# RWKV-6 attention and a GELU MLP: the last tile's first product by seven half products, and a new order at the start

## The chip, the cores and the metric

The kernel runs on one core of one Trainium2 chip. A core has a matrix engine (TensorE, PE in the profile, with its weight loads shown apart as PEld), a vector engine (VectorE, DVE), a scalar engine (ScalarE, ACT), GpSimd (POOL) and a queue engine that issues DMAs (SyncE, SP). Each engine works through its own queue in order, and waits for the others by semaphores. Matmuls write only to PSUM, an on-chip buffer of eight banks of 512 fp32 columns; VectorE and ScalarE read the results from there. The metric is the device time of one execution in microseconds (us); less is better. 13 runs of the kernel before gave a median of 614.05 us (610.53 to 616.07).

## The reference

Two stages: a linear attention with a decaying state per head (RWKV-6), and an MLP with the exact GELU on its output.

```python
for t in range(S):                                   # per batch and head
    cur = np.einsum('bhd,bhe->bhde', u[None] * kt, vt)
    y[:, :, t] = np.einsum('bhd,bhde->bhe', rt, state + cur)
    state = wt[:, :, :, None] * state + np.einsum('bhd,bhe->bhde', kt, vt)
...
h = x @ w_in                                         # x: y as (3072, 384)
g = 0.5 * h * (1.0 + erf(h * inv_sqrt2))
return (g @ w_out).astype(np.float32)
```

Sizes: batch 4, 8 heads, 768 steps, head size 48, so x is 3072 x 384; w_in is 384 x 2048, w_out 2048 x 384. The weights come as float64 and are turned into fp32 on the chip; everything is computed in fp32.

## The kernel before

The 3072 rows are cut into eight tiles x = 0 to 7 of T = 384 steps. For each tile `attention(x, unit)` makes x transposed (`xT`, three chunks of 128 of the 384 inputs by 384 rows), and `mlp(x)` multiplies it by w_in (h, line 723), applies GELU (line 726) into `g`, and multiplies by w_out. Both are Python generators: each `yield` ends a piece of work, and the loop at line 902 pulls the pieces of `mlp(x - 1)` one by one (a "step") and puts pieces of the next tile's attention between them, at the steps that the lists `place` and `place_next` name. The order in which the code runs is the order in every engine's queue; semaphores are placed by the framework from the tiles that an instruction reads and writes.

**h of a tile** (lines 718 to 739): sixteen groups f of 128 of the 2048 columns; each takes three fp32 matmuls of 128 x 128 by 384 columns, over the three chunks, into a PSUM tile `h_ps` of one bank (two such buffers, tag "mm"), and one GELU.

**The product with w_out** for tiles from 1 on (lines 768 to 810): two of the three blocks of 128 rows are multiplied by seven products of halves in place of eight (Strassen's way in Winograd's form), with sums of g in `s1`, `s2`, `s3` (lines 730 to 738) and sums of w_out made once (`w_sums`). Each product is eight matmuls of 192 columns. The third block of an odd tile waits and is paired with that of the even tile after it; that of the last tile is alone and is multiplied plainly at the very end (lines 849 to 865: 16 matmuls of 384 columns, a copy on VectorE, a store of 192 KB).

**Tile 0's attention** runs in two units of two head pairs each, before any MLP work; `units.reverse()` at line 885 puts unit 1 (pairs 2 and 3) first for the last pieces. Those are: the state chain on VectorE (lines 602 to 618), the first half of y with a small "fence" copy on VectorE (lines 630 to 634), and the second half of y (line 648), whose results are copied to xT: unit 0 by lines 653 to 657, unit 1's pair 3 through `ysb` and six DMAs (lines 671 to 676), and its pair 2 by two VectorE copies (line 669). Then the conversion of weights (`convert`, 16 pieces, VectorE lines 303 to 310, ScalarE lines 291 and 292) is mixed with the steps of `mlp(0)` and with tile 1's attention. In that attention `halves` makes six levels; at each, matmuls (line 402) go to a tile `d`, VectorE scales r (line 437) and writes to a_sb under a mask (line 447); the diagonal is one more set of products (lines 409 and 413).

**From tile 2 on** the attention uses `quarters`: ScalarE and VectorE lay out r in kx (lines 488, 493, 494), then come small matmuls (508, 515) at step 8 and step 13, VectorE scales and masked copies (522 to 553), the state chain at step 18 and the two halves of y at steps 20 and 21. PSUM tiles of the attention have two banks each, tag "d", three buffers: together with the two of tag "mm" they fill the eight banks.

Of the kernel before, what the change touches and what calls it, by code (L numbers as in the profile page):

```python
# [10 lines left out]
F32 = mybir.dt.float32  # L11
# [5 lines left out]
AF = mybir.ActivationFunctionType  # L17
# [6 lines left out]
T = 384  # L24
# [7 lines left out]
BANK = 512  # L32
# [12 lines left out]
def kernel(  # L45
# [25 lines left out]
    nc = tc.nc  # L71
    NX = rkw.shape[0]
    NP = u.shape[1]
    NPART = NP // Q
    N_TOK, DM = out.shape
    HALVES = 2
    NJ = DM // 128
    DF = w_in.shape[1]
    NF = DF // 128
# [4 lines left out]
    io = ctx.enter_context(tc.tile_pool(name="io", bufs=2))  # L84
    wk = ctx.enter_context(tc.tile_pool(name="wk", bufs=2))
# [15 lines left out]
    ALL = NP * T  # L101
# [85 lines left out]
    def keep_warm(n):  # L187
        t = ps.tile([128, BANK], F32, name="warm", tag="mm", bufs=2) if n else None
        for _ in range(n):
            nc.tensor.matmul(t, lhsT=zeros[:, 0:128], rhs=zeros, start=True, stop=True)  # L190
# [121 lines left out]
    xT_of = {}  # L312

    def attention(x, unit):
# [346 lines left out]
        for b in reversed(range(np_)):  # L661
            for q in reversed(range(Q)):
                pair = parts[b] * Q + q
                y = ys[b][:, :, q * N3 * C:(q + 1) * N3 * C].rearrange("p c (i t) -> p c i t", t=C)
                if pair < NJ:
                    for z in range(2):
                        s = slice(z * G, z * G + D)
                        copy = nc.vector.tensor_copy if x == 0 else nc.scalar.copy
                        copy(out=xT[s, pair, :].rearrange("p (i c t) -> p c i t", c=2, t=C), in_=y[s])
                    continue  # L670
                ysb = wk.tile([128, T], F32, name="ysb", bufs=1)
                nc.scalar.copy(out=ysb.rearrange("p (i c t) -> p c i t", c=2, t=C), in_=y)
                for z in range(2):
                    for j in range(NJ):
                        e = z * G + j * (G - D)
                        (nc.scalar if z * NJ + j > (2 if x == 0 else 3) else nc.sync).dma_start(out=xT[z * G + D:(z + 1) * G, j, :], in_=ysb[e:e + G - D, :])
# [12 lines left out]
    def w_sums():  # L689
# [3 lines left out]
        for i, (x, y) in enumerate((((0, 1), (0, 0)), ((1, 1), 0), ((1, 1), (0, 1)), ((1, 0), 1))):  # L693
            for k in range(2):
                ks = slice(k * FG, (k + 1) * FG)
                nc.vector.tensor_sub(sums[i][:, ks], w_quarter(*x, k), sums[y][:, ks] if isinstance(y, int) else w_quarter(*y, k))
                yield

    def mlp(x):


# [12 lines left out]
        def new_sums(tag):  # L714
            return cv.tile([128, FG, 128], F32, name="s", tag=tag)

        s1, s2, s3 = [], [], []
        for n, group in enumerate((0, 2, 1, 3) if halves else range(4)):
            gs[group] = gp.tile([128, FG, T], F32, name="g")
            for f in range(group * FG, (group + 1) * FG):  # L720
                h_ps = ps.tile([128, BANK], F32, name="h_ps", tag="mm", bufs=2)[:, 0:T]
                for j in range(NJ):
                    nc.tensor.matmul(h_ps, lhsT=w_in_sb[:, f // FI, j, f % FI * 128:(f % FI + 1) * 128], rhs=xT[:, j, :],  # L723
                                     start=(j == 0), stop=(j == NJ - 1))
                t = T - 128 if waits else T
                nc.scalar.activation(out=gs[group][:, f % FG, 0:t], in_=h_ps[:, 0:t], func=AF.Gelu)  # L726
                if waits:
                    nc.scalar.activation(out=alone[:, f], in_=h_ps[:, t:], func=AF.Gelu)

                if halves and n == 3 and f % FG >= FG - 2:  # L730
                    k = f % FG - FG + 2
                    for s, tag in ((s1, "f"), (s2, "e")):
                        s.append(new_sums(tag))
                    s3.append(s3_sb[0][:, k * FG:(k + 1) * FG])
                    a00, a10, a11 = (gs[g][:, :, a:a + 128] for g, a in ((k, 0), (k, 128), (k + 2, 128)))
                    nc.vector.tensor_add(s1[k], a10, a11)  # L736
                    nc.vector.tensor_sub(s2[k], s1[k], a00)
                    nc.vector.tensor_sub(s3[k], a00, a10)
                yield

        def product(o, lhs, rhs, start=False):
# [19 lines left out]
        def psum():  # L761
            return ps.tile([128, BANK], F32, name="o_ps", tag="mm", bufs=2)[:, 0:HM]

        def two_rows():
            return [wk.tile([128, DM], F32, name="o_sb", bufs=2) for _ in range(2)]


        if halves:
# [44 lines left out]
        if waits:  # L813
            _, o2, o1 = psum(), psum(), psum()
            o_sb = wk.tile([128, DM], F32, name="o_sb", bufs=2)
            product(o2, of_alone(0), of_w(0, 0), True)
            nc.scalar.copy(out=p1_alone, in_=o2)
            yield
            product(o1, of_alone(1), of_w(1, 0), True)
            nc.vector.tensor_add(o_sb[:, 0:HM], o1, p1_alone)  # L820
            store(row0 + 256, o_sb[:, 0:HM])
            yield
        elif ends:
            o_sb = two_rows()
            p1, u2, u3 = p1_alone, *(wk.tile([128, HM], F32, name=name, bufs=1) for name in ("u2", "u3"))
            o2, o1 = psum(), psum()
            product(o1, of_blocks(2, 1), of_t(3), True)
            nc.scalar.copy(out=o_sb[1][:, 0:HM], in_=o1)
            yield
            product(o2, of_sums(s2), of_t(1), True)  # L830
            nc.vector.tensor_add(u2, o2, p1)
            yield
            product(o1, of_sums(s1), of_t(0), True)
            nc.scalar.copy(out=o_sb[1][:, HM:], in_=o1)
            for k in range(2):
                nc.vector.tensor_sub(s2[k], alone[:, HF + k * FG:HF + (k + 1) * FG], s2[k])
            yield
            product(o2, of_sums(s3), of_t(2))
            nc.vector.tensor_add(u3, o2, p1)
            for c in range(2):  # L840
                z = o_sb[1][:, c * HM:(c + 1) * HM]
                nc.vector.tensor_add(z, z, u3)
            store(row0 + 256, o_sb[1])
            yield
            product(o1, of_sums(s2), of_w(1, 1))
            nc.vector.tensor_add(o_sb[0][:, 0:HM], o1, u2)
            store(row0 - T + 256, o_sb[0][:, 0:HM], HM)
            yield
        else:

            if halves:
                psum()
            for blocks in ((2,),) if halves else ((0, 1), (2,)):
                o_ps = [ps.tile([128, BANK], F32, name="o_ps", tag="mm", bufs=2)[:, 0:DM] for _ in blocks]
                for f in range(NF):
                    for i, o in zip(blocks, o_ps):
                        nc.tensor.matmul(o, lhsT=block(i, f // HF, f % HF), rhs=w_out_sb[:, f, :],  # L857
                                         start=(f == 0), stop=(f == NF - 1))
                    if (not halves or f % 4 == 3) and f < NF - 1:
                        yield  # L860
                for i, o in zip(blocks, o_ps):
                    o_sb = wk.tile([128, DM], F32, name="o_sb", bufs=2)
                    nc.vector.tensor_copy(out=o_sb, in_=o)
                    store(x * T + i * 128, o_sb)
                yield
# [23 lines left out]
    for _ in shares:  # L889
        pass  # L890
    convert()
    for unit, warm in zip(units, ((1, 2, 1), (0, 0, 5))):
        for n in warm:
            next(unit)
            keep_warm(n)
    convert()
    slots = attention(1, 0)
    next(slots)
# [2 lines left out]

    for x in range(1, NX):

        place = [1, 2, 4, 7, 9, 11, 13, 15, 18, 20, 26, 32] if x == 1 else [1, 6, 8, 13, 15, 16, 18, 18, 20, 21]
        place_next = [38, 47] if x == 1 else [21, 24] if x % 2 == 0 else [25, 27]
        loads = load(x + 1, nc.scalar if x > 1 else nc.sync)

        times = range(20, 30) if x == 1 else (2, 3, 4, 5, 16, 17, 18, 19, 20, 21)
        following = attention(x + 1, 0) if x + 1 < NX else iter(())
        more = iter(())  # L910
        for step, _ in enumerate(mlp(x - 1)):
            if x == 1 and step == 2 * NF - 2:

                make_quarter_masks()
                more = w_sums()
            next(more, None)
            if x == 1 and step in (0, 2, 4, 6, 8, 10, 12, 14, 15, 17, 18, 20, 22, 24):
                convert()
            if step in times:
                next(loads, None)  # L920
            while place and place[0] <= step:
                place.pop(0)
                next(slots, None)
            while place_next and place_next[0] <= step:
                place_next.pop(0)
                next(following, None)
        for _ in slots:
            pass
        slots = following
# [62 lines left out]
```

## Time and profile before

| | us |
|---|---|
| median of 13 runs | 614.05 |
| the profiled execution | 614.72 |
| its span, first to last instruction | 612.9 |
| TensorE busy | 592.9 |
| VectorE busy | 448.3 |
| ScalarE busy | 173.5 |
| start to the first h matmul | 50.05 |
| first h matmul of the last tile | 549.65 |
| its h, in the chain that ended last | 30.96 |
| its seven products | 18.20 |
| its third block | 10.33 |

The page gives for each engine its busy time, and then the chain of work that ended last, followed back from the last instruction. The timeline lists instructions in order of time, merged where they are alike; in brackets is the idle time of the engine before them and what ended it. The granted TensorE clock was 0.999 of full speed over the run.

### The profile page before, as it was taken

What the parts mean: (1) busy time and instruction counts of PE and PEld (TensorE: products, weight loads), DVE (VectorE), ACT (ScalarE), POOL (GpSimd) and SP (SyncE); (2) the same over time, 40 slices, a digit from 0 to 9 for tenths busy, and PEclk for the clock granted to TensorE, in tenths of its full rate; (3) what the DMA queues carried; (4) which work ended last, traced back from release to release, by engine and by line L of the source; (5) the groups of instructions that cost most, each with busy time, mean ns of one, the idle gap of its engine ahead of it and who ended that gap; (6) DMA issues with size and microseconds to landing.
All of it is one profiled execution on the core that took longest, in us unless ns stands there. A gap on an engine that the chain in (4) does not pass through costs nothing.

```text
span 612.9 us, 15812 instructions
## 1 busy us (share of the span) xinstructions
PE 592.9 (97%) x6917; PEld 446.5 (73%) x6935; DVE 448.3 (73%) x801; ACT 173.5 (28%) x389; POOL 8.4 (1%) x24
## 2 busy tenths in 40 slices
PE   8768899999999999999999999999999999999997
PEld 4455566566699568996689668995789668995694
DVE  7868999999885988679776888569786888520120
ACT  2236367123322232113222232023322132022200
POOL 3100000000000000000000000000000000000000
PEclk9999999999999999999999999999999999999999
DMA  5756358203042303213052203213052002010001
GB/s 195 212 202 206 109 158 290 76 30 91 2 110 72 97 1 77 89 35 90 2 109 72 75 24 74 88 39 91 3 107 73 8 2 40 18 40 0 1 1 40
DMA packets 50565, 46.71 MB, mean 76 GB/s; under 512 B 31680, under 2 KB 35904, under 8 KB 50496
## 3 DMA queue, kind: packets, MB, share of 16 engines
q1 hardware_dynamic: 33152, 29.31, 15.8%
q10 hardware_dynamic: 17344, 16.39, 9.9%
q8 instruction: 55, 0.90, 0.6%
q14 instruction: 14, 0.11, 0.1%
HBM read 36.24 MB, written 4.72 MB: 67 GB/s over the span
## 4 chain that ended last, share of the span: by engine, by line
PE 81%; DVE 13%; issue 3%; DMA 2%; ACT 1%; SPq 0%; DVEq 0%
PE h_ps L723 35%; PE o_ps L743 29%; PE d L515 4%; PE o_ps L857 4%; DVE e L306 2%; DVE rkw L437 2%; PE y_ps L648 2%; PE kv_ps L592 2%; PE y_ps L630 2%; DVE a_sb L447 1%; DVE w_out_sb L310 1%; DMA rkw<-kx 1%; DMA rkw<-in_rkw_dram 1%; PE d L508 1%; PE d L402 1%
## 5 line engine op out<-in xcount | busy, mean ns | idle before, releaser
L723 PE MATMUL h_ps<-xT,w_in_sb 128*128 128x384 f32 x768 | 254.2, 489 | 1.2 <-ACT f L291 1.2
L723 PEld LDWEIGHTS h_ps<-xT,w_in_sb 128*128 128x128 f32 x768 | 144.1, 190 | 98.3 <-ACT f L291 1.7
L726 ACT ACTIVATE g<-h_ps 128x384 f32<-128x384 f32 (+1 forms) x128 | 57.3, 450 | 198.8 <-PE h_ps L723 198.8
L743 PE MATMUL o_ps<-t,s 128*128 128x192 f32 x480 | 81.9, 329 | 0.0
L743 PEld LDWEIGHTS o_ps<-t,s 128*128 128x128 f32 x480 | 77.8, 190 | 0.7
L546 DVE COPY_PREDICATED a_sb<-quarter,d 128x384 f32<-128x384 uint8 (+2 forms) x108 | 45.0, 438 | 2.5
L857 PE MATMUL o_ps<-w_out_sb,g 128*128 128x384 f32 x128 | 43.0, 490 | 0.1
L743 PE MATMUL o_ps<-w_out_sb,g 128*128 128x192 f32 x224 | 38.7, 326 | 0.0
L743 PEld LDWEIGHTS o_ps<-w_out_sb,g 128*128 128x128 f32 x224 | 37.0, 190 | 1.9
L857 PEld LDWEIGHTS o_ps<-w_out_sb,g 128*128 128x128 f32 x128 | 23.7, 190 | 16.7 <-DVE w_out_sb L310 1.0
L736 DVE TENSOR_TENSOR s<-g 128x512 f32<-128x512 f32 x14 | 9.4, 670 | 29.1 <-ACT g L726 29.1
L402 PEld LDWEIGHTS d<-rkw 64*64 64x64 f32 x1152 | 19.0, 136 | 13.9 <-issue 7.0
L743 PE MATMUL o_ps<-w_out_sb,s 128*128 128x192 f32 x160 | 28.3, 330 | 0.0
L743 PE MATMUL o_ps<-t,g 128*128 128x192 f32 x160 | 27.6, 326 | 0.0
L402 PE MATMUL d<-rkw 64*64 64x64 f32 (+1 forms) x1152 | 21.5, 223 | 6.2 <-DVE a_sb L447 2.5
L339 DVE TRANSPOSE_TENSOR_REDUCE rkw<-kx 128x48 f32<-128x1536 f32 (+3 forms) x24 | 26.8, 1155 | 0.2
L515 PEld LDWEIGHTS d<-kx,rkw 64*64 64x64 f32 x1152 | 24.3, 133 | 3.4 <-DVE a_sb L553 1.6
L515 PE MATMUL d<-kx,rkw 64*64 64x96 f32 x1152 | 26.5, 245 | 0.0
L743 PEld LDWEIGHTS o_ps<-t,g 128*128 128x128 f32 x160 | 26.3, 190 | 0.0
L743 PEld LDWEIGHTS o_ps<-w_out_sb,s 128*128 128x128 f32 x160 | 25.9, 190 | 0.4
L528 DVE TENSOR_TENSOR rkw<-rkw,tot_sb 128x768 f32<-128x768 f32 x12 | 11.5, 958 | 17.4 <-PE d L515 17.4
L375 DVE TENSOR_TENSOR rkw<-rkw 128x384 f32<-128x384 f32 (+2 forms) x24 | 23.6, 1008 | 0.4
(117 smaller groups left out, 642.4 us busy)
## 6 DMA issues: line engine op xcount, KB each, us to landing
rkw<-in_rkw_dram ACTq DMA_DIRECT2D x45, 256.0 KB, 2.8
raw<-in_w_out_dram SPq DMA_DIRECT2D x8, 768.0 KB, 4.5
out_dram<-o_sb SPq DMA_DIRECT2D x21, 192.0 KB, 1.9
raw<-in_w_in_dram SPq DMA_DIRECT2D x5, 768.0 KB, 5.4
v_in<-in_v_dram ACTq DMA_DIRECT2D x5, 584.0 KB, 3.7
raw<-in_w_in_dram SPq DMA_DIRECT2D x9, 256.0 KB, 4.1
rkw<-in_rkw_dram SPq DMA_DIRECT2D x8, 288.0 KB, 3.6
rkw<-in_rkw_dram SPq DMA_DIRECT2D x9, 256.0 KB, 7.4
```

The lines of the kernel that those rows point to most:

```text
L306: nc.vector.scalar_tensor_tensor(out=e, in0=hi, scalar=0x80000000, in1=e, op0=ALU.bitwise_and, op1=ALU.bitwise_or)
L339: nc.vector.tensor_reduce(out=fine_sb[:, e, 0:n].rearrange("p a n -> p (a n)"), in_=kx[:, o:o + n * n_m].rearrange("p (m j) -> p m j", j=3 ...
L375: nc.vector.tensor_mul(z, z, by)
L402: nc.tensor.matmul(d[half[p], g, n * width:(n + 1) * width], lhsT=kc[half[g], b, i, p], rhs=right(half[g], b, i, p), start=True, stop=True)
L437: nc.vector.tensor_mul(rk, rk, tt)
L515: nc.tensor.matmul(d[half[p], g, i * 3 * C // 2:(i + 1) * 3 * C // 2], lhsT=kc[half[g], (n + i) // NI, (n + i) % NI, p], rhs=rx[half[g], 2 ...
L546: nc.vector.copy_predicated(out=an[:, :, :, :, (a + 1) * h:], mask=mask.to_broadcast(data.shape), data=data)
L592: nc.tensor.matmul(kv_ps[half[g], p, i * D:(i + 1) * D], lhsT=k_t(b, i, p, g), rhs=vs(b, i, g)[half[p], 0:D], start=True, stop=True)
L723: nc.tensor.matmul(h_ps, lhsT=w_in_sb[:, f // FI, j, f % FI * 128:(f % FI + 1) * 128], rhs=xT[:, j, :], start=(j == 0), stop=(j == NJ - 1))
L726: nc.scalar.activation(out=gs[group][:, f % FG, 0:t], in_=h_ps[:, 0:t], func=AF.Gelu)
L743: nc.tensor.matmul(o, lhsT=lhs(j), rhs=rhs(j), start=start and j == 0, stop=(j == HF - 1), skip_group_check=True)
L857: nc.tensor.matmul(o, lhsT=block(i, f // HF, f % HF), rhs=w_out_sb[:, f, :], start=(f == 0), stop=(f == NF - 1))
```

## The change

At the start, unit 1 of tile 0 yields once more, between the copies of pair 3 and of pair 2, and the last pieces of the two units are pulled in another order: unit 0's state chain comes before the copies of unit 1's pair 2. In the list `place` for tile 1 the steps 2 and 4 become 3 and 5.

For the last tile, h is computed for its 384 rows in two halves of 192 columns: over the first two of the three chunks of inputs, pairs of groups (f and f + 8) take seven products of halves in place of eight, and the third chunk is added plainly, four matmuls, in the same accumulations. That is eleven matmuls of 192 columns for a pair, where there were six of 384. `h_sums` makes the sums of w_in (eight VectorE operations of 128 x 512) and of x (four of 128 x 192) during the steps of the tile before; `h_halves` issues the matmuls and the additions into six PSUM banks, taken as three tiles of two banks. `of_g` holds the sums of g that stood inline. The third block's product is moved ahead of the seven products, with its last two f at its end.

The diff, without blank lines and the parts that only re-indent:

```diff
@@ attention
         for b in reversed(range(np_)):
             for q in reversed(range(Q)):
                 pair = parts[b] * Q + q
+                if x == 0 and pair == NP - 2:
+                    yield
@@ after w_sums
+    HT = T // 2
+    in_s, in_t = [], []
+    def h_sums():
+        n = DF // 2
+        rest = io.tile([128, v.shape[2]], F32, name="v_in")
+        for z in (bufs[0][:, 0:n], rest[:, 0:n], kx[:, 0:n], bufs[1][:, ALL:ALL + n]):
+            in_s.append(z.rearrange("p (i c) -> p i c", c=WI))
+        hi = DF // WI // 2
+        def w(a, c, k):
+            return w_in_sb[:, a * hi + k * hi // 2:a * hi + (k + 1) * hi // 2, c, :]
+        def s(i, k):
+            return in_s[i - 1][:, k * hi // 2:(k + 1) * hi // 2]
+        for i in range(4):
+            for k in range(2):
+                if i == 0:
+                    nc.vector.tensor_add(s(1, k), w(1, 0, k), w(1, 1, k))
+                elif i == 1:
+                    nc.vector.tensor_sub(s(2, k), s(1, k), w(0, 0, k))
+                elif i == 2:
+                    nc.vector.tensor_sub(s(3, k), w(0, 0, k), w(1, 0, k))
+                else:
+                    nc.vector.tensor_sub(s(4, k), w(0, 1, k), s(2, k))
+                yield
+        in_t.extend(tot_sb[:, i * HT:(i + 1) * HT] for i in range(4))
+        xT = xT_of[NX - 1]
+        x00, x01, x10, x11 = (xT[:, c, b * HT:(b + 1) * HT] for c in range(2) for b in range(2))
+        nc.vector.tensor_sub(in_t[0], x01, x00)
+        nc.vector.tensor_sub(in_t[1], x11, in_t[0])
+        yield
+        nc.vector.tensor_sub(in_t[2], x11, x01)
+        nc.vector.tensor_sub(in_t[3], x10, in_t[1])
+        yield
@@ mlp
+        def of_g(k):
+            for s, tag in ((s1, "f"), (s2, "e")):
+                s.append(new_sums(tag))
+            s3.append(s3_sb[0][:, k * FG:(k + 1) * FG])
+            a00, a10, a11 = (gs[g][:, :, a:a + 128] for g, a in ((k, 0), (k, 128), (k + 2, 128)))
+            nc.vector.tensor_add(s1[k], a10, a11)
+            yield
+            nc.vector.tensor_sub(s2[k], s1[k], a00)
+            yield
+            nc.vector.tensor_sub(s3[k], a00, a10)
+            yield
+        def h_halves():
+            banks = [ps.tile([128, 2, BANK], F32, name="d", tag="d", bufs=3) for _ in range(3)]
+            b_1, b_6, b_7, b_5, b_4, b_0 = (z[:, i, 0:HT] for z in banks for i in range(2))
+            temps = [bufs[1][:, 2 * ALL + i * HT:2 * ALL + (i + 1) * HT] for i in range(8)]
+            x00, x01, x10, x11 = (xT[:, c, b * HT:(b + 1) * HT] for c in range(2) for b in range(2))
+            more = iter(())
+            for f in range(HF):
+                k = f // FG
+                if f % FG == 0:
+                    for group in (k, k + 2):
+                        gs[group] = gp.tile([128, FG, T], F32, name="g")
+                p1, u2, u3 = (wk.tile([128, HT], F32, name=name, bufs=1) for name in ("p1", "u2", "u3"))
+                u5, c12, c21, c22 = temps[f % 2::2]
...
+                last = [xT[:, 2, b * HT:(b + 1) * HT] for b in range(2)]
+                multiply(b_1, (w(0, 0), x00))
+                nc.scalar.copy(out=p1, in_=b_1)
+                multiply(b_6, (s(2), in_t[1]))
+                nc.vector.tensor_add(u2, b_6, p1)
+                multiply(b_7, (s(3), in_t[2]))
+                nc.vector.tensor_add(u3, b_7, u2)
+                multiply(b_5, (s(1), in_t[0]))
+                nc.vector.tensor_add(u5, b_5, u3)
+                multiply(b_1, (w(0, 1), x10), (w(0, 2), last[0]), start=False)
+                gelu(0, 0, b_1)
+                multiply(b_4, (w(1, 1), in_t[3]), (w(1, 2), last[0]))
+                nc.vector.tensor_add(c21, b_4, u3)
+                gelu(1, 0, c21)
+                multiply(b_0, (w(1, 2), last[1]))
+                nc.vector.tensor_add(c22, b_0, u5)
+                gelu(1, 1, c22)
+                multiply(b_5, (s(4), x11), (w(0, 2), last[1]), start=False)
+                nc.vector.tensor_add(c12, b_5, u2)
+                gelu(0, 1, c12)
+                next(more, None)
+                if f % FG == FG - 1:
+                    more = of_g(k)
+            for _ in more:
+                pass
...
+        final = x == NX - 1
+        if final:
+            h_halves()
-        for n, group in enumerate((0, 2, 1, 3) if halves else range(4)):
+        for n, group in enumerate(() if final else (0, 2, 1, 3) if halves else range(4)):
...
+        if final:
+            o_ps = ps.tile([128, BANK], F32, name="o_ps", tag="mm", bufs=2)[:, 0:DM]
+            order = [f for f in range(NF) if f % HF < HF - 1] + [HF - 1, NF - 1]
+            for n, f in enumerate(order):
+                nc.tensor.matmul(o_ps, lhsT=block(2, f // HF, f % HF), rhs=w_out_sb[:, f, :], start=(n == 0), stop=(n == NF - 1))
+            o_sb = wk.tile([128, DM], F32, name="o_sb", bufs=2)
+            nc.scalar.copy(out=o_sb, in_=o_ps)
+            store(x * T + 256, o_sb)
+            yield
...
-        else:
-            if halves:
-                psum()
-            for blocks in ((2,),) if halves else ((0, 1), (2,)):
+        elif not final:
+            for blocks in (0, 1), (2,):
@@ the order at the start
-    for unit, warm in zip(units, ((1, 2, 1), (0, 0, 5))):
-        for n in warm:
-            next(unit)
-            keep_warm(n)
+    for unit, n in ((0, 1), (0, 2), (0, 1), (1, 0), (0, 0), (1, 0), (1, 4)):
+        next(units[unit])
+        keep_warm(n)
@@ the loop over tiles
-        place = [1, 2, 4, 7, 9, 11, 13, 15, 18, 20, 26, 32] if x == 1 else [1, 6, 8, 13, 15, 16, 18, 18, 20, 21]
+        place = [1, 3, 5, 7, 9, 11, 13, 15, 18, 20, 26, 32] if x == 1 else [1, 6, 8, 13, 15, 16, 18, 18, 20, 21]
...
-            next(more, None)
+            if x == NX - 1 and step == 2:
+                more = h_sums()
+            if x < NX - 1 or step in (2, 3, 4, 5, 17, 19, 22, 23, 24, 26):
+                next(more, None)
```

More of the change, by code (lines that the diff above doesn't have):

```diff
@@ new lines, in h_halves, with w, s, multiply @@
+        def h_halves():
[11 more added lines that the diff above has]
+                u5, c12, c21, c22 = temps[f % 2::2]
+                def w(a, j):
+                    g = a * HF + f
+                    return w_in_sb[:, g // FI, j, g % FI * 128:(g % FI + 1) * 128]
+                def s(i):
+                    return in_s[i - 1][:, f // FI, f % FI * 128:(f % FI + 1) * 128]
+                def multiply(o, *factors, start=True):
+                    for i, (lhsT, rhs) in enumerate(factors):
+                        nc.tensor.matmul(o, lhsT=lhsT, rhs=rhs, start=start and i == 0, stop=(i == len(factors) - 1),
+                                         skip_group_check=True)
+                def gelu(a, b, z):
+                    nc.scalar.activation(out=gs[2 * a + k][:, f % FG, b * HT:(b + 1) * HT], in_=z, func=AF.Gelu)
+                last = [xT[:, 2, b * HT:(b + 1) * HT] for b in range(2)]
[23 more added lines that the diff above has]
+                pass
@@ L730, in mlp @@
                 if halves and n == 3 and f % FG >= FG - 2:
[L731 to L738, printed above, removed]
+                    for _ in of_g(f % FG - FG + 2):
+                        pass
                 yield
@@ L858, in mlp @@
                                          start=(f == 0), stop=(f == NF - 1))
-                    if (not halves or f % 4 == 3) and f < NF - 1:
+                    if f < NF - 1:
                         yield
```

## The prediction

> **What bounds the kernel now.** I read the page first (busy shares, then the chain that ended last), then the timeline of the last tile, of the tile before it and of the start, where the change works.
>
> ```profile
> PE 592.9 (97%) x6917; PEld 446.5 (73%) x6935; DVE 448.3 (73%) x801; ACT 173.5 (28%) x389; POOL 8.4 (1%) x24
> PE 81%; DVE 13%; issue 3%; DMA 2%; ACT 1%; SPq 0%; DVEq 0%
> ```
>
> TensorE is 81% of the chain; VectorE's 13% is nearly all in the first 118 us, where it converts weights. So a stall of TensorE after 118 us is paid in full, and before that VectorE's chain is what counts. The timeline of the last tile (start, length, engine, line; in brackets the idle time before and its releaser):
>
> ```profile
> 549.65 31.12 PE L723 MATMUL h_ps<-xT,w_in_sb 128*128 128x384 f32 x96
> 555.66 0.49 ACT L726 ACTIVATE g<-h_ps 128x384 f32<-128x384 f32 x1 [1.44 <-PE h_ps L723]
> ...
> 583.41 0.32 ACT L774 COPY p<-o_ps 128x192 f32<-128x192 f32 x1 [2.11 <-PE o_ps L743]
> ...
> 588.41 7.96 PE L743 MATMUL o_ps<-t,s 128*128 128x192 f32 x48
> ...
> 596.41 0.36 DVE L792 TENSOR_TENSOR u<-o_ps,p 128x192 f32<-128x192 f32 x1 [3.57 <-PE o_ps L743]
> ...
> 598.81 10.48 PE L857 MATMUL o_ps<-w_out_sb,g 128*128 128x384 f32 x32
> ...
> 609.34 0.56 DVE L863 COPY o_sb<-o_ps 128x384 f32<-128x384 f32 x1 [9.96 <-PE o_ps L857]
> ```
>
> There are two hardware instructions to one fp32 matmul of the code (96 for 16 x 3). The chain has L723 at 30.96 us for 96, so 0.3225 us each, and L743 at 18.20 for 112, so 0.1625 each: a matmul of 192 columns costs 0.325 us, half of one of 384. A reader of PSUM starts 0.20 us after the slot of the last matmul ends (596.21 to 596.41); a copy of 192 columns takes 0.32 on ScalarE, an add 0.36 on VectorE. TensorE idles nowhere in this stage.
>
> The start, where VectorE has the lead:
>
> ```profile
> 42.38 0.48 ACT L672 COPY ysb<-y_ps 128x384 f32<-128x384 f32 x1 [3.16 <-PE y_ps L648]
> ...
> 42.89 1.12 DVE L669 COPY xT<-y_ps 48x384 f32<-48x384 f32 x2 [2.21 <-ACT ysb L672]
> 44.03 0.26 DVE L617 COPY st<-kv_ps 128x96 f32<-128x96 f32 x1
> 44.32 1.84 DVE L606 SCALAR_TENSOR_TENSOR st<-st,tot_sb,kv_ps 128x48 f32<-128x48 f32 x10
> ...
> 46.08 0.15 DVE L634 COPY fence<-y_ps 128x2 f32<-128x2 f32 x1
> ...
> 46.29 1.38 PE L648 MATMUL y_ps<-rkw,st 64*64 64x64 f32 x40 [2.78 <-DVE fence L634]
> ...
> 47.72 0.96 ACT L656 COPY xT<-y_ps 48x384 f32<-48x384 f32 x2 [4.86 <-PE y_ps L648]
> ...
> 48.71 1.12 DVE L656 COPY xT<-y_ps 48x384 f32<-48x384 f32 x2 [2.48 <-ACT xT L656]
> ```
>
> Two things: VectorE idles 2.21 us before L669 although the state chain (L617, L606) behind it had its inputs at 37.5 (the kv matmuls of 36.61 had ended). And the second L656 waits for the first, although ScalarE reads the first bank of that y_ps and VectorE the second. The writes aren't the reason: they interleave without overlap in xT, and the next view shows such writes running at once. So **the program's waits hold a PSUM tile of two banks as one thing**: an access to one bank waits for another engine's access to the other.
>
> The tile before the last (kx is written there by L488 and L493, interleaved, and both start at 492.54):
>
> ```profile
> 492.54 1.34 ACT L488 COPY kx<-rkw 128x384 f32<-128x384 f32 x3 [1.74 <-DVE rkw L375]
> 492.54 0.56 DVE L493 TENSOR_TENSOR kx<-rkw,tot_sb 128x384 f32<-128x384 f32 x1
> 493.50 0.96 DVE L494 TENSOR_TENSOR kx<-kx,tot_sb 128x768 f32<-128x768 f32 x1 [0.40 <-ACT kx L488]
> ...
> 494.08 1.06 PE L508 MATMUL d<-rkw 64*128 64x48 f32 x16
> ...
> 495.07 2.21 PE L515 MATMUL d<-kx,rkw 64*64 64x96 f32 x96
> ```
>
> VectorE works from 476.83 to 494.46 without a gap but that of 0.40, and L515 needs L494: only 0.6 us of slack there.
>
> **What the Trainium skill says.** "Perfetto Trace Analysis", Matmuls: independent matmul groups should rotate through PSUM banks, so that the evacuation of one overlaps the next. L723 does so (two tiles of one bank), and shows no idle TensorE. "PSUM — Partial Sum Buffer", Terms: two engines on one bank at once is an error, reads included. That explains L669 behind L672 (same banks), not the two L656, which sit in different banks; there the trace decides.
>
> **The change, part by part.**
>
> *Start.* The chain of the second unit moves ahead of L669: it runs from 40.70 (after the first unit's fence, 40.52+0.16) to 42.83, inside the old gap; L669 still starts at 42.89 and ends at 44.01; the fence comes at 44.03, not 46.08, and L648 at 44.25, not 46.29 (its other input, L630, is done by 43.5). Both L656 and the conversion behind them follow: 2.04 us earlier. ScalarE's xT DMAs are issued by 45.03, before its L656 at 45.68; the last lands about 2.2 later, 47.2, before h starts at 48.0. One warm-up matmul fewer lies in idle time. From there to 118 VectorE is the chain and keeps its order, since steps 3 and 5 fall between the same conversions (even steps) as 2 and 4. TensorE gets one h group ahead of each moved slot, which removes its 1.59 us wait at 65.03, but it then waits for the next L437 instead: nothing more. **-2.04.**
>
> *Tile before the last.* h_sums puts four VectorE operations of 128x512 at steps 2 to 5, behind L375 and ahead of L493. L736 to L738 have this form: 0.61 us from one to the next. 4 x 0.61 = 2.44, so L493 starts at 495.0, L494 at 495.54 and ends at 496.50 (the gap of 0.40 is swallowed). L515 starts at 496.56, not 495.07. **+1.49**, all of it TensorE, and all behind it shifts together. Bounds: 0 if these operations found a gap, 2.4 if the gap of 0.40 stays. The later ones lie in idle time: s3 ahead of L610 (520.93 to 521.54, and L615 waits for kv until 522.08), then behind L783, with 1.16 idle before the fence; s4 and in_t between 538 and 549, in gaps of 3.64, 3.64 and 1.53.
>
> *h of the last tile.* Per pair of f: 11 matmuls of 192 for 12, 3.575 us; eight make 28.60 against 30.96, 2.36 less, if nothing waits. But banks are paired b_1+b_6, b_7+b_5, b_4+b_0, each a tile "d" of the kind seen in L656. In program order TensorE then waits three times per f (0.05 us from release to restart, as from ScalarE's 2.24 to the first warm-up at 2.29):
> - b_6 after the copy of b_1. That copy stands on ScalarE behind the gelu of c12 of the f before: last b_5 slot ends at 0; +0.20+0.36 (c12) +0.03+0.33 (gelu; 0.27 for 128 columns, 0.38 for 256) +0.32 (copy) +0.05 = 1.29, where b_6 was due at 0.325: **0.96** (in the first f, with ScalarE free, 0.20+0.32+0.05 = 0.57).
> - second b_5 product after u3 (reads b_7). b_6 ends at 1.615, +0.20+0.36 (u2), +0.03+0.36 (u3), +0.05 = 2.615; due at 1.94: **0.67**.
> - b_0 after c21 (reads b_4): 0.20+0.36+0.05 = **0.61**.
>
> Sum 2.24 per f. Restart: L723's first twelve after a pause take 4.11 where 11 x 0.3225+0.489 = 4.04, so 0.07 each; bounds 0 and 0.19 (a whole weight load, PEld's mean). Period 3.575+2.24+0.21 = 6.03; first 5.64; total 5.64+7 x 6.03 = 47.9. Against 30.96: **+16.9** (15.2 to 19.8). The sums of of_g (0.65 each) fall behind c12, while VectorE waits for b_6. VectorE's six adds and ScalarE's five operations, 2.2 and 1.6 us per f, are no bound by themselves.
>
> *Rest.* The third block's product (10.33) moves ahead of the seven (18.20): same work; its 14 first matmuls (9 us) cover the last gelus. The end is an add of 0.36 in place of the copy of 0.56, with a store of the same size: **-0.2**.
>
> Sum: -2.04+1.49+16.9-0.2 = +16.2 on the profiled execution's 614.72 us (span 612.9). The median of the runs shown is 614.05, so **630.2 us**.
>
> **Rivals.**
> 1. *Banks are held apart* (faster): the wait of the second L656 comes from xT after all. Then no wait in h binds: the copy of b_1 ends at 1.24, before the accumulation at 1.30. -2.04+1.49-2.36-0.2 = -3.1: 611.0. For it: the copies do write one xT. Against: L488 and L493. It decides as soon as b_6 need not wait for the copy of b_1; even 0.4 us per f would eat it.
> 2. *Each restart costs a full weight load*: 24 x 0.12 = +2.9: 633.1. For it: no view shows 128x128 weights loaded ahead over a wait.
> 3. *The start gives nothing*: another input of h is late (its idle of 1.20 there is put down to ScalarE's L291, which is none of its inputs), or weights' DMAs hold the earlier conversions: 632.2.
> 4. *The pairing holds only in part*, so that one of the three waits is missing (b_0's, 0.61+0.07 per f, is the cheapest): 8 x 0.68 = 5.4 less, 624.8. For it: L656 shows two readers, not a matmul behind a reader of the other bank.
>
> **How the numbers follow.** Forecast 0.70, rival 2 0.11, rival 3 0.07, rival 4 0.04, rival 1 0.08. The range 626 to 634.5 holds the forecast with its bounds and rivals 2 and 3; rivals 1 and 4 stay out. About 0.2% is what a measurement can tell from no change. Only rival 1 is faster: 0.08 faster, 0.01 same, 0.91 slower.
>
> **What would show it.** In the last tile: TensorE's 176 matmuls of h over about 48 us, with three idle gaps in each of eight periods, released by ScalarE's copy to p1 and VectorE's adds. In the tile before: L515 about 1.5 us later against h's start, released by VectorE. At the start: h at 48.0. I am wrong if h takes under 35 us, which would mean that the paired banks run free.

## The result, and the profile after

The changed kernel takes 629.72 us in the median of 11 runs (627.66 to 633.14), the kernel before 613.99 in 48 runs. The medians differ by 15.7 us. The ratio, which is taken from all runs and not from the two medians, is 1.0273, with a 95% interval of 1.0254 to 1.0292: about 16.8 us slower. The forecast was 630.2 us, with a range of 626 to 634.5.

The page of the changed kernel, for the two lines that were shown of before:

```profile
PE 596.7 (95%) x6996; PEld 456.0 (73%) x7014; DVE 470.9 (75%) x860; ACT 179.3 (29%) x414; POOL 8.4 (1%) x24
PE 65%; DVE 5%; DMA 1%; issue 1%; ACT 1%; DVEq 0%; ACTq 0%
```

TensorE's busy share fell from 97% to 95% while the span grew from 612.9 to 626.9 us. Its busy time says little here, since the listed times of matmuls overlap (a pair is listed with 0.49 us, and the next can start 0.325 us after it); the waits say it. The second line can't be set beside that of the kernel before: its shares add up to 73% only, because the chain of this profile is followed back no further than to 166.13 us. This is the view of waits of the changed kernel for TensorE in the last tile, from 546 to 595 us (who waited for whom: total us, times, longest); the kernel before has none in its last h:

```profile
PE d L798 <- ACT p L806: 5.5, 8, 0.7
PE d L798 <- DVE u L810: 4.7, 8, 0.6
PE d L798 <- DVE rkw L816: 3.6, 8, 0.5
```

Three waits, eight times each. The timeline of one period (the second pair of groups, from b_6 on), with TensorE's matmuls and the readers of PSUM, shows what they wait for:

```profile
552.05 0.36 DVE L822 TENSOR_TENSOR rkw<-d,u 128x192 f32<-128x192 f32 x1 [0.29 <-PE d L798]
552.44 0.36 ACT L802 ACTIVATE g<-rkw 128x192 f32<-128x192 f32 x1 [0.29 <-DVE rkw L822]
552.71 0.30 ACT L806 COPY p<-d 128x192 f32<-128x192 f32 x1
...
553.07 0.59 PE L798 MATMUL d<-tot_sb,v_in 128*128 128x192 f32 x2 [0.73 <-ACT p L806]
...
553.49 0.49 PE L798 MATMUL d<-tot_sb,kx 128*128 128x192 f32 x2
...
554.16 0.36 DVE L810 TENSOR_TENSOR u<-d,u 128x192 f32<-128x192 f32 x1
...
554.57 0.59 PE L798 MATMUL d<-tot_sb,rkw 128*128 128x192 f32 x2 [0.59 <-DVE u L810]
...
556.50 0.36 DVE L816 TENSOR_TENSOR rkw<-d,u 128x192 f32<-128x192 f32 x1 [0.94 <-PE d L798]
...
556.91 0.59 PE L798 MATMUL d<-xT,w_in_sb 128*128 128x192 f32 x2 [0.45 <-DVE rkw L816]
...
557.34 0.49 PE L798 MATMUL d<-xT,rkw 128*128 128x192 f32 x2
...
559.21 0.59 PE L798 MATMUL d<-tot_sb,v_in 128*128 128x192 f32 x2 [0.73 <-ACT p L806]
```

The matmul at 553.07 writes b_6, and no operand of it comes from L806, which copies b_1 to p1. It starts 0.06 us after that copy has ended. The one at 554.57 writes b_5 and waits for the reader of b_7, the one at 556.91 writes b_0 and waits for the reader of b_4: each time the other bank of the same tile. From 553.07 to 559.21 the period is 6.14 us, of which 3.575 are work. The figure in brackets is the idle time against the listed end of the pair before. Counted from where that pair's 0.325 us end, the three waits are 0.90, 0.755 and 0.61 us.

At the start, the order of VectorE has changed as the diff says, and h starts 5.65 us after the ysb copy (45.25 less 39.60), where it was 7.67 (50.05 less 42.38):

```profile
39.60 0.48 ACT L675 COPY ysb<-y_ps 128x384 f32<-128x384 f32 x1 [1.60 <-PE y_ps L648]
...
40.12 1.12 DVE L672 COPY xT<-y_ps 48x384 f32<-48x384 f32 x2 [0.15 <-ACT ysb L675]
41.27 0.16 DVE L634 COPY fence<-y_ps 128x2 f32<-128x2 f32 x1
...
41.48 1.38 PE L648 MATMUL y_ps<-rkw,st 64*64 64x64 f32 x40 [0.75 <-DVE fence L634]
...
45.25 4.11 PE L839 MATMUL h_ps<-xT,w_in_sb 128*128 128x384 f32 x12 [1.41 <-ACT f L291]
```

The copy's own 2.78 us earlier start is not the change's: in the experiments below it starts between 38.4 and 41.5 us with these same instructions ahead of it, and at 39.9 in a kernel that lacks the change at the start. So positions in two traces are compared from a common event, not from zero.

In the tile before the last, L515 now waits for L494:

```profile
488.79 1.06 PE L508 MATMUL d<-rkw 64*128 64x48 f32 x16
489.58 0.55 DVE L493 TENSOR_TENSOR kx<-rkw,tot_sb 128x384 f32<-128x384 f32 x1
490.23 0.96 DVE L494 TENSOR_TENSOR kx<-kx,tot_sb 128x768 f32<-128x768 f32 x1
...
491.44 2.21 PE L515 MATMUL d<-kx,rkw 64*64 64x96 f32 x96 [1.59 <-DVE kx L494]
```

It starts 2.65 us after L508, where that was 0.99 before: 1.66 us lost. The last tile's h runs from 546.03 to 594.84, 48.81 us for 30.96 (17.85 lost). From the start of that h to the end of the span it is 80.87 us for 63.25, 17.62 more, so the end gave back 0.23. With the start's 2.02: 17.62 + 1.66 - 2.02 = 17.3 us, inside the interval of the ratio (15.6 to 17.9). The two profiled executions themselves differ by 14.0 us (626.9 less 612.9): the 17.3, less the 2.78 by which the copy happened to be early, and less some 0.5 us by which the tiles between the start and the tile before the last went faster, which isn't explained.

### The profile page after: what moved, and what is told of

Its sections match the earlier page's. It is cut to its first block, busy times and chain, and to the rows that moved or that the text cites. A ratio compares the mean times of both kernels' runs of the same rounds, so it can differ in the third digit from the quotient of the medians.

```text
span 626.9 us, 16084 instructions
## 1 busy us (share of the span) xinstructions
PE 596.7 (95%) x6996; PEld 456.0 (73%) x7014; DVE 470.9 (75%) x860; ACT 179.3 (29%) x414; POOL 8.4 (1%) x24
## 4 chain that ended last, share of the span: by engine, by line
PE 65%; DVE 5%; DMA 1%; issue 1%; ACT 1%; DVEq 0%; ACTq 0%
PE o_ps L853 28%; PE h_ps L839 22%; PE d L798 5%; PE d L515 3%; PE o_ps L882 2%; PE kv_ps L592 2%; PE y_ps L630 1%; PE y_ps L648 1%; DMA rkw<-kx 1%; DVE rkw L375 1%; DVE kx L346 1%; PE d L508 1%; DVE u L808 0%; DVE u L810 0%; DVE rkw L816 0%
## 5 line engine op out<-in xcount | busy, mean ns | idle before, releaser
L839 PE MATMUL h_ps<-xT,w_in_sb 128*128 128x384 f32 x672 | 223.0, 489 | 1.4 <-ACT f L291 1.4
L839 PEld LDWEIGHTS h_ps<-xT,w_in_sb 128*128 128x128 f32 x672 | 125.9, 190 | 86.0 <-ACT f L291 1.9
L842 ACT ACTIVATE g<-h_ps 128x384 f32<-128x384 f32 (+1 forms) x112 | 49.4, 444 | 169.4 <-PE h_ps L839 169.4
L853 PEld LDWEIGHTS o_ps<-w_out_sb,g 128*128 128x128 f32 x224 | 37.0, 190 | 1.9
L976 PE MATMUL o_ps<-w_out_sb,g 128*128 128x384 f32 x96 | 32.7, 493 | 0.2
L515 PE MATMUL d<-kx,rkw 64*64 64x96 f32 x1152 | 26.5, 245 | 1.6 <-DVE kx L494 1.6
L515 PEld LDWEIGHTS d<-kx,rkw 64*64 64x64 f32 x1152 | 24.3, 133 | 5.0 <-issue 3.3
L976 PEld LDWEIGHTS o_ps<-w_out_sb,g 128*128 128x128 f32 x96 | 17.7, 190 | 13.1 <-DVE w_out_sb L310 1.4
L798 PE MATMUL d<-xT,w_in_sb 128*128 128x192 f32 x96 | 21.8, 335 | 3.6 <-DVE rkw L816 3.6
L488 ACT COPY kx<-rkw 128x384 f32<-128x384 f32 x36 | 16.1, 509 | 27.7 <-PE d L515 17.3
```

Source lines behind the costliest of these rows:

```text
L488: nc.scalar.copy(out=z, in_=r4[:, :, :, f, :])
L515: nc.tensor.matmul(d[half[p], g, i * 3 * C // 2:(i + 1) * 3 * C // 2], lhsT=kc[half[g], (n + i) // NI, (n + i) % NI, p], rhs=rx[half[g], 2 ...
L798: nc.tensor.matmul(o, lhsT=lhsT, rhs=rhs, start=start and i == 0, stop=(i == len(factors) - 1), skip_group_check=True)
L853: nc.tensor.matmul(o, lhsT=lhs(j), rhs=rhs(j), start=start and j == 0, stop=(j == HF - 1), skip_group_check=True)
```

## The experiments

Seven kernels, each an edit of the changed kernel or of the kernel before. Those of one group were run on one chip beside runs of the kernel before, whose median there is given: 613.65 us for the accumulators apart, the later sums, both, and the pairing in the kernel before; 611.97 us for the other three. The changed kernel itself belongs to neither group, so it is compared by the ratios, not by the medians.

### The accumulators apart

```diff
+            single = [ps.tile([128, BANK], F32, name="h_ps", tag="mm", bufs=2) for _ in range(2)]
-            b_1, b_6, b_7, b_5, b_4, b_0 = (z[:, i, 0:HT] for z in banks for i in range(2))
+            b_1, b_5 = (z[:, 0:HT] for z in single)
+            b_7, b_4, b_6, b_0 = (z[:, i, 0:HT] for z, i in ((banks[0], 0), (banks[1], 0), (banks[2], 0), (banks[2], 1)))
```

The matmuls, additions and GELUs are the same in number and order. b_6 and b_0 still share a tile, but between one's reader and the other's matmul there is time enough.

> The changed kernel with the six accumulators of the last tile's h in tiles so that no matmul waits for a reader of another bank: b_1 and b_5 in the two one-bank tiles of tag mm, b_7 and b_4 alone in their tiles, b_6 and b_0 together. Theory A (waits between paired banks make the loss): the three stalls per f go, h takes 28.6 to 29.0 us in place of 48.8, the time is 614.0-2.0+1.65-2.36-0.2 = 611.1 us, about 18.6 below the changed kernel and about 0.5% below the kernel before. Rival B (the chain of additions u2, u3, u5, c21, c22, c12 and ScalarE's order bind by themselves, whatever the banks): h stays above 40 us, the time above 622. Rival C (matmuls of 192 columns with changing weights and accumulators cost more in themselves): h between 31 and 36 us without idle stretches in front of single matmuls, 614 to 618.

Measured: 610.64 us (22 runs), ratio to before 0.9947 (0.9928 to 0.9966). The timeline of the second pair of groups in that kernel, TensorE and the first two readers:

```profile
550.12 0.49 PE L800 MATMUL d<-tot_sb,v_in 128*128 128x192 f32 x2
...
550.45 0.49 PE L800 MATMUL d<-tot_sb,kx 128*128 128x192 f32 x2
...
550.66 0.30 ACT L808 COPY p<-h_ps 128x192 f32<-128x192 f32 x1
550.77 0.49 PE L800 MATMUL h_ps<-tot_sb,rkw 128*128 128x192 f32 x2
550.99 0.36 DVE L810 TENSOR_TENSOR u<-d,p 128x192 f32<-128x192 f32 x1 [0.64 <-ACT p L808]
...
551.10 0.83 PE L800 MATMUL h_ps<-xT,w_in_sb 128*128 128x192 f32 x4
```

b_6, b_7 and b_5 follow each other at 0.325 us, and b_6's matmul (550.12) starts before the copy of b_1 (550.66) instead of behind it. The copy comes no earlier than in the changed kernel (0.54 us after the end of b_1's matmuls in both), but b_6 no longer waits for it. The next matmul into b_1 (551.10) must wait for it, since it adds to what the copy reads, and comes 0.14 us after the copy's end: there is little to spare. TensorE waits nowhere in this h, which takes 28.79 us. So theory A holds; rivals B and C are out. Of the losses only the wait of L515 is left here, and it costs more in this trace than in that of the changed kernel:

```profile
490.02 3.45 PE L515 MATMUL d<-kx,rkw 64*64 64x96 f32 x96 [1.59 <-DVE kx L494]
```

The same matmuls take 2.21 us there. The granted TensorE clock is 0.50 from 491.02 to 494.02 here, and 1.00 around the same place in the changed kernel's trace. From the start of L515 to the last tile's h it is 56.20 us for 54.59: another 1.61 us lost.

### One pair parted

```diff
-            b_1, b_6, b_7, b_5, b_4, b_0 = (z[:, i, 0:HT] for z in banks for i in range(2))
+            b_1, b_6, b_7, b_5, _, b_0 = (z[:, i, 0:HT] for z in banks for i in range(2))
+            b_4 = ps.tile([128, BANK], F32, name="h_ps", tag="mm", bufs=2)[:, 0:HT]
```

> The changed kernel with one of the three pairs parted: b_4 in a one-bank tile, so that b_0 need not wait for c21; the pairs b_1+b_6 and b_7+b_5 stay. Theory A (each pair costs by itself): the wait of b_0 (0.61 us and a restart of 0.10) goes in each of eight periods, 5.7 us less than the changed kernel, 624.0, and two idle stretches per period stay. Rival (the waits overlap, so that what one gives up the next takes): less than 2 us, above 627.7.

Measured: 625.17 us (6 runs), ratio 1.0214 (1.0187 to 1.0241). Its waits over the whole run keep two of the three, at the same size:

```profile
PE d L799 <- ACT p L807: 5.5, 8, 0.7
PE d L799 <- DVE u L811: 4.7, 8, 0.6
```

And its period, between two matmuls of b_6:

```profile
553.63 0.59 PE L799 MATMUL d<-tot_sb,v_in 128*128 128x192 f32 x2 [0.73 <-ACT p L807]
...
559.06 0.59 PE L799 MATMUL d<-tot_sb,v_in 128*128 128x192 f32 x2 [0.73 <-ACT p L807]
```

5.43 us for 6.14: 0.71 less, the 0.61 of the wait and 0.10 of the restart, as expected. The whole h takes 43.08 us (547.31 to 590.39) for 48.81, 5.73 less. So the waits add up and do not hide each other. The times of the runs show less of it. Against the changed kernel, the ratio is lower by 0.0059, some 3.6 us, with an interval from 1.6 to 5.6, which by itself would not rule out the rival. Part of the difference can be the lowered clock behind L515, which this trace shows too (L515 takes 3.26 us, and again 1.61 us are lost up to h).

### The pairing without the seven products

```diff
                 h_ps = ps.tile([128, BANK], F32, name="h_ps", tag="mm", bufs=2)[:, 0:T]
+                if x == NX - 1:
+                    if n == 0 and f == 0:
+                        pair_of_banks = ps.tile([128, 2, BANK], F32, name="d", tag="d", bufs=3)
+                    h_ps = pair_of_banks[:, f % 2, 0:T]
```

(in the kernel before; the first line serves the other tiles)

> The kernel before with one edit: the last tile's sixteen groups of h go in turn to the two banks of one tile of two banks, in place of two tiles of one bank. Nothing else changes: same matmuls, same GELUs, no additions. Theory A (a PSUM tile of two banks is held as one thing, so a group waits for the GELU of the group before though that reads the other bank): per group 0.20+0.49+0.05+0.10 = 0.84 us of idle TensorE, fifteen times 12.6 us, 626.6. Rival B (banks of one tile are held apart and the stalls of the changed kernel come from its own chain of additions): 614.0, no idle.

Measured: 626.68 us (4 runs), ratio 1.0200 (1.0152 to 1.0248). Its timeline in the last tile's h, from the first GELU on:

```profile
550.51 0.49 ACT L731 ACTIVATE g<-d 128x384 f32<-128x384 f32 x1 [6.82 <-PE d L728]
...
551.05 2.20 PE L728 MATMUL d<-xT,w_in_sb 128*128 128x384 f32 x6 [0.58 <-ACT g L731]
553.29 0.49 ACT L731 ACTIVATE g<-d 128x384 f32<-128x384 f32 x1 [2.29 <-PE d L728]
...
553.84 2.20 PE L728 MATMUL d<-xT,w_in_sb 128*128 128x384 f32 x6 [0.58 <-ACT g L731]
```

A group writes one bank, the GELU reads the other, and still the group waits until the GELU has ended. 2.79 us from group to group where it was 1.935 (6 x 0.3225): 0.855 for an expected 0.84. Fifteen such waits make 12.8 us, and the medians differ by 13.0 (613.65 to 626.68). This is the kind of wait that the change brought, without any of its arithmetic, so the pairing alone makes such a loss.

### The sums of w_in later

```diff
-            if x < NX - 1 or step in (2, 3, 4, 5, 17, 19, 22, 23, 24, 26):
+            for _ in range(1 if x < NX - 1 else {22: 5, 25: 5}.get(step, 0)):
                 next(more, None)
```

> The changed kernel with all ten pieces of h_sums moved to steps 22 and 25 of the tile before, five at each, where VectorE was seen idle. Theory A (the four sums at steps 2 to 5 delay L494 and so L515): the stall of 1.65 us before L515 goes, 1.65 us faster than the changed kernel, 628.1. Rival B (the stall is covered by a later wait of TensorE, so the place of the sums is worth nothing): 629.7, same as the changed kernel. Rival C (at steps 22 and 25 they delay the products that need s2, or the first matmuls of h): a new idle stretch between 540 and 552, slower than 629.7.

Measured: 628.41 us (5 runs), ratio 1.0236 (1.0195 to 1.0276). By the ratios that is 2.3 us less than the changed kernel, but the intervals overlap and can't tell it from no gain. The timeline can:

```profile
490.77 1.06 PE L508 MATMUL d<-rkw 64*128 64x48 f32 x16
...
491.76 2.21 PE L515 MATMUL d<-kx,rkw 64*64 64x96 f32 x96
```

L515 is back at 0.99 us behind L508, with no wait. That it is a gain in time is seen better without the larger loss, in the next run.

### Both

The two edits together.

> Both edits: accumulators apart and the sums late. If the two losses are independent: 611.1-1.65 = 609.5 us, 0.7% below the kernel before, and h of 28.6 to 29.0 us. If either loss only hid the other: not below the better of the two single edits.

Measured: 608.23 us (6 runs), ratio 0.9907 (0.9872 to 0.9943). It beats the kernel before by 5.4 us in the group's medians, and the single edits too (610.64 and 628.41), so neither loss only hid the other. Its h is made of 176 matmuls that follow each other, 28.80 us from the first to the product behind it:

```profile
545.16 0.49 PE L800 MATMUL h_ps<-xT,w_in_sb 128*128 128x192 f32 x2
...
573.64 0.49 PE L800 MATMUL h_ps<-xT,w_in_sb 128*128 128x192 f32 x2
573.96 10.48 PE L884 MATMUL o_ps<-w_out_sb,g 128*128 128x384 f32 x32
```

Against the accumulators apart alone, the later sums give 2.4 us (1.4 to 3.3, an interval worked out from the spread of the two kernels' runs), where 1.65 was expected. If more than that is real, the clock can account for it. In 13 of the 22 executions of that kernel the mean granted clock is 0.997 or less, about what one such stretch of half clock makes of a mean; in the eleven of the two kernels with late sums it is never below 0.999. An estimate from these counts: 1.66 us, and 1.61 us in 13 of 22 executions, make 2.6 us on average. Which executions had the stretch behind L515 isn't recorded, so this is not shown.

### The start alone, and the start without the moved steps

The kernel before with the extra yield and the new order of the two units; in the first of the two also with steps 3 and 5 for 2 and 4.

```diff
+                if x == 0 and pair == NP - 2:
+                    yield
-    for unit, warm in zip(units, ((1, 2, 1), (0, 0, 5))):
-        for n in warm:
-            next(unit)
-            keep_warm(n)
+    for unit, n in ((0, 1), (0, 2), (0, 1), (1, 0), (0, 0), (1, 0), (1, 4)):
+        next(units[unit])
+        keep_warm(n)
```

> The kernel before with only the edits at the start: the extra yield, the new order of the two units, and steps 3 and 5 in place of 2 and 4. Theory A: VectorE's chain starts 2.0 us earlier and keeps the lead until 118 us, so 2.0 us less than before, ratio 0.9967. Rival (something else, a DMA of weights or TensorE, takes the lead by 118 us): less than 0.7 us.

> The kernel before with the extra yield and the new order of the units, but the old steps 2 and 4. Theory A: the moved steps are worth nothing, so the same time as with them, ratio 0.9967. Rival (the moved steps carry the gain, by the 1.59 us that TensorE no longer waits): as before, ratio 1.000, or up to 1.6 us slower than with both.

Measured, 22 runs each beside 43 of the kernel before (611.97): with the steps 609.95, ratio 0.9971 (0.9954 to 0.9988); without them 609.77, ratio 0.9963 (0.9946 to 0.9980). The new order gives the 2.0 us that were expected, and the moved steps give nothing that can be measured. In the changed kernel's trace TensorE indeed does not wait at the level where it waited 1.59 us before (65.03 there, 60.51 here), and waits at the next instead:

```profile
60.51 1.60 PE L402 MATMUL d<-rkw 64*64 64x32 f32 x96
62.04 4.14 PE L839 MATMUL h_ps<-xT,w_in_sb 128*128 128x384 f32 x12
66.83 1.60 PE L402 MATMUL d<-rkw 64*64 64x32 f32 x96 [0.66 <-DVE rkw L437]
```

The kernel with the old steps keeps that wait (1.58 us at 59.23 in its trace) and is no slower. So the wait cost nothing that shows.

## Why the prediction was right

It named the decisive cost and its size, for the reason that the runs then showed.

- *Start*, -2.04: 2.02 from the ysb copy to h in the trace, and 2.0 in the medians of the start alone. The moved steps at nothing: confirmed, with the wait found again one level later, as said.
- *Tile before the last*, +1.49: 1.66 in the trace. Two terms were short: L494 starts 0.65 after L493 and not 0.55, and L515 starts 0.25 after L494 ends, where 0.06 was taken. Against that, L493 came 0.13 earlier behind L508 than forecast. The later sums cost nothing that shows. That the clock could drop behind this wait was not in the prediction.
- *h of the last tile*, +16.9: 17.85. The first wait was given as 0.57 and is 0.57 (slot end 546.355 to 546.92); from the second pair on it is 0.90 for 0.96, because the copy starts 0.27 after the GELU ahead of it on ScalarE, not 0.33. The second is 0.755 for 0.67, since a VectorE addition that needs the one before it starts 0.46 and not 0.39 behind it. The third is 0.61 for 0.61. A restart costs 0.10, not 0.07. Sum 3.575 + 2.265 + 0.31 = 6.15 for a measured 6.14; forecast was 6.03.
- *End*, -0.2: 0.23 given back.

The medians differ by 15.7 us, 0.5 less than the 16.2 of the forecast; the terms in the trace add up to 17.3, which is 1.1 more, nearly all of it in h. That the median came so close is therefore in part luck. The mechanism is not.

The reading behind it, that a PSUM tile of two banks is held as one thing, came from a single row, the second L656, and from the reasoning that interleaved writes to kx ran at once. It needed a test, since that row shows two readers; the pairing put into the kernel before shows it for a matmul behind a reader. The releasers in these views are inferred from semaphore events, which speaks for waits that the program sets, but no run here tests it; with the banks in separate tiles the wait is gone. One reading of the prediction was too wide: the Trainium skill's "PSUM — Partial Sum Buffer", Terms, calls it an error when two engines are on the same bank and the same group of 32 partitions at once, not on the same bank alone. In the kernel before, L672 reads all 128 partitions, so what was said of L669 there stands: it starts 0.03 us after L672 has ended. No run here shows such an error.

Rival 1 was wrong for this kernel, but it described what the change does once the accumulators stand apart: 611.0 was worked out for it, and 610.64 measured. Rivals 2, 3 and 4 did not come: a restart is 0.10 and not 0.19, the start gave its 2 us, and all three waits are there.

## What to carry to other kernels

Where the waits go by tile, as in this program, give accumulators that are read while others are written a PSUM tile each, or pair only those whose accesses are far apart in time; count waits by tile, not by bank. An arithmetic saving of 2.4 us in a stage where TensorE never idles is worth having only if no new wait enters it: with 0.3 us of wait per pair of groups it would have been gone. And work that is added "in the shadow" belongs where the timeline shows the engine idle (here steps 22 and 25), not where it is merely off TensorE.

## What the runs showed of the hardware

One fp32 matmul of the code is a pair of instructions. With 128 x 128 weights and 192 columns a pair starts 0.325 us after the one before it in a stream, with new weights for each (550.12, 550.45, 550.77 with the accumulators apart). Behind a wait the next pair starts 0.42 to 0.43 us later (553.07 to 553.49, 556.91 to 557.34), so a restart costs 0.10.

A GELU or copy of 192 columns on ScalarE is listed with 0.30 to 0.36 us, but the next can start 0.27 us after it (552.44 to 552.71).

The granted clock of TensorE fell to 0.50 for some 3 us in three of the nine traces. Each had a wait of TensorE there: 1.59 us before L515 with the accumulators apart, 1.58 with one pair parted, and 2.78 before L648 at the start of the kernel before with the pairing, where L648 takes 2.40 us for 1.38 and h starts 1.0 us later behind the ysb copy. In the traces of the changed kernel and of the kernel before, the same waits have no such drop behind them. What decides isn't shown. Where such a drop came with a wait, TensorE lost more than the wait itself.

The ysb copy, at the same place in the program, starts between 38.4 and 42.4 us in the nine traces, and at 42.4 and 39.9 in the two with the old start. A single execution can thus be some us early or late for reasons that are not the kernel's; what share of the spread of the times this makes was not measured.
